# Fewer weight conversions in the first heads' turns, more in the next stage's, one normalisation on VectorE, fewer unread products

## The chip, the cores and the metric

The kernel runs on one core of a Trainium2 chip. TensorE multiplies, VectorE (DVE) and ScalarE (ACT) do element-wise work, GpSimd (POOL) does a little of it and the indirect transfers, and SyncE (SP) issues most DMA transfers. Each engine works through its own instructions in program order, and semaphores hold an instruction back until its inputs are there. The metric is the device time of one execution in microseconds (us), lower is better.

## The reference, cut to what matters

Three blocks in a row: attention with a window of 128 and four sink positions, a feed-forward block with squared relu, and a mixture of eight experts of which each token uses two.

```python
scores = scale * np.matmul(q, k.transpose(0, 1, 3, 2))      # 2 x 8 heads, 768 x 768
scores = np.where(keep, scores, -1000000000.0)              # window or sink
a = softmax(scores); x = np.matmul(a, v)                    # -> 1536 tokens x 512
h = x @ w_in; r = np.maximum(h, 0.0); g = r * r; x = g @ w_out   # 512 -> 2048 -> 512
# gate: top 2 of 8 experts per token; each expert relu(x @ w1[e]) @ w2[e]
```

The weights `w_in` and `w_out` come as float64 and are turned into float32 in the kernel by integer operations on VectorE.

## The kernel before, in words

All of attention and of the squared-relu block is in the function `fast1`. The tokens are cut into six groups of 256 (g), each with eight heads, so that there are 48 pairs of a head and a group, called heads a = 0 to 47 below. The squared-relu block of a group has eight units u of 256 hidden columns, so there are 48 of these too, n = 8g + u.

The work is laid out by hand in the order of the program. First come the **turns of the first heads**, a loop over a = 0 to 11 (lines 717 to 755). In turn a

- TensorE makes the scores of head a + 1 (line 270, tile `s`), some unread products of ones that keep it busy (line 706, their number is in W1), in every second turn the product of two earlier heads with v (`pv`, line 352, tile `o`), and the transposes of head a - 1 (lines 326 to 330, tile `pt`);
- VectorE takes masked score and maximum of head a (line 292, two instructions), in every second turn the low part of `pv`'s result (line 358), and adds and inverts the sums of head a - 1 (lines 299 and 301);
- ScalarE takes the exponentials of head a (line 295), copies the transposes of head a - 2 (line 336), multiplies head a - 1 by the inverse sums in two halves t = 0 and t = 1 (line 311; half 0 has 128 columns up to head 7, half 1 has 256, from head 8 on both have 264), and copies `pv`'s result (line 357).

H0 says by a letter for each half which engine multiplies: "a" is ScalarE, "d" is VectorE (line 313).

Then comes the **squared-relu loop** over n (line 764). In turn n TensorE makes the scores of head n + 11, in even turns `pv`, then `mm1(n + 1)` (line 425, 24 products into `h`), the transposes of head n + 10, and `mm2(n)` (line 462). In turn 5 two small transposes (line 376) and in turn 6 the sink products (line 399) stand ahead of `mm1`. `mm1(n + 1)` reads the first weights of unit n + 1 as a high part `w` and a low part `wl`:

```python
for c in range(4):
    for a, b in PASS:                  # (0, 0), (0, 1), (1, 0)
        PE.matmul(hp[:, f], w[a][:, c * 256 + f * 128:c * 256 + f * 128 + 128], x[:, b, c],
```

So the third product of each c is the one that reads `wl`. A weight tile is made in two halves; c = 0 and 1 lie in its first half, c = 2 and 3 in its second, and the ninth product of `mm1` is the first that reads the second half of `wl`.

The **conversion** of these weights fills VectorE. There are 32 halves (for each u two of `w_in` and two of `w_out`). Each takes three instructions, called steps here: line 196, line 199 and line 202. A half of `w_in` is then rounded to its high part by ScalarE (line 205) and takes one step more, the subtraction at line 180 that writes half of `wl`. That makes 14 steps a unit and 112 in all, in a fixed list; `convert(k)` issues the next k of them at the place where it stands. The step at line 202 frees the loaded half, and a load of 512 KB three halves further on is then issued on SP's queue. The low part of unit u is complete with step 14u + 10.

The tables say how many steps stand where. In turn a of the first heads C0[a] has the number ahead of the sums of head a - 1 and the number behind them (in turn 0 only the first is issued). In turns n = 0 to 7 of the squared-relu loop C1[n] has four numbers: behind the maxima, between the sum and its inverse, behind the inverse, and behind the instructions of `act(n + 1)`.

Of the kernel before, what the change touches and what calls it, by code (L numbers as in the profile page):

```python
# [34 lines left out]
def build(tc, io):  # L35
# [3 lines left out]
    with root:  # L39
# [47 lines left out]
        wk = ph1.enter_context(tc.tile_pool(name="wk", bufs=2))  # L87
        ps = psst.enter_context(tc.tile_pool(name="ps", bufs=2, space=PSUM))
        ex = fast1(tc, io, locals())
        ph1.close()  # L90
        ph2 = ExitStack()
# [9 lines left out]
def fast1(tc, io, env):  # L101
# [70 lines left out]
    def convert(count):  # L172

        for _ in range(min(count, len(todo))):
            i, c = todo.pop(0)
            name, u, hf = cvs[i]
            sl = slice(hf * 512, hf * 512 + 512)
            if c == "L":
                w = W[name, u]
                DVE.tensor_tensor(w[1][:, sl], CV.pop(i).bitcast(F32), w[0][:, sl].bitcast(F32), op=OP.subtract)  # L180
                if hf:
                    split.add((name, u))
                continue
            wd = ST[i].bitcast(I32).rearrange("p (n t) -> p n t", t=2)
            if c == "1":
                if name == "win":
                    if hf == 0:
                        W[name, u] = env["halves"]()
                    t = CV[i] = cvp.tile([128, 512], I32, name="cv", bufs=3)
                else:  # L190
                    if hf == 0:

                        RAW[name, u] = spare.tile([128, 1024], F32, name="rw0") if u == 7 else \
                            ring.tile([128, 1024], F32, name="wl")
                    t = CV[i] = RAW[name, u][:, sl].bitcast(I32)
                DVE.tensor_scalar(t, wd[:, :, 1], 0x07FFFFFF, 3, op0=OP.bitwise_and, op1=OP.logical_shift_left)
            elif c == "2":
                t = CV[i]
                DVE.scalar_tensor_tensor(t, wd[:, :, 1], -1073741824, t, op0=OP.bitwise_and, op1=OP.bitwise_or)
            else:  # L200
                t = CV[i]
                DVE.scalar_tensor_tensor(t, wd[:, :, 0], 29, t, op0=OP.logical_shift_right, op1=OP.bitwise_or)
                del ST[i]
                if name == "win":
                    ACT.copy(W[name, u][0][:, sl], t.bitcast(F32))
                elif hf:
                    made.add((name, u))
                cv_load()
# [89 lines left out]
    def norm_a(a, sm, between=0):  # L298
        DVE.tensor_scalar(sm[:, 0:2], sm[:, 0:2], 1.0e-9, None, op0=OP.add)
        convert(between)  # L300
        DVE.reciprocal(sm[:, 2:4], sm[:, 0:2])

    def norm(a, sm, how):
        g, h = divmod(a, 8)
        p = PR[a]
        for t in range(2):
            sc = sm[:, 2 + t:3 + t]
            lo, hi = span(a, t)
            pt = p[:, t, lo:hi]
            if how[t] == "a":  # L310
                ACT.activation(pt, pt, AF.Copy, scale=sc)
            else:
                (DVE if how[t] == "d" else POOL).tensor_scalar(pt, pt, sc, None, op0=OP.mult)  # L313
        if g % 3:
            if h == 0:
                PSK[g] = wk.tile([128, 2, 64], F32, name="psk", bufs=1)
            for t in range(2):
                o = 128 + 128 * t
                POOL.tensor_copy(PSK[g][:, t, h * NS:h * NS + NS], p[:, t, o:o + NS])  # L319
# [96 lines left out]
    def mm1(n):  # L416
        g, u = divmod(n, 8)
        hp = ps.tile([128, 2, 256], F32, name="h")
        assert ("win", u) in split
        x, w = XT[g], W["win", u]  # L420
        for f in range(2):
            i = 0
            for c in range(4):
                for a, b in PASS:
                    PE.matmul(hp[:, f], w[a][:, c * 256 + f * 128:c * 256 + f * 128 + 128], x[:, b, c],  # L425
                              start=i == 0, stop=i == 11)
                    i += 1
        HP[n] = hp
# [256 lines left out]

    A0 = 11
    PLAIN = tuple(range(18))
    C0 = ((1, 1),) + ((2, 1),) * 11
    H0, H1, H2 = "aa", "aa", "dd"
    C1 = ((3, 1, 4, 4),) * 8  # L690
    smv = {}
    HALF, V1 = 18, (5, 6, 7)
    W0, W1 = 20, (6, 5) + (4,) * 9

    with tc.manual_schedule():
        cvst = ExitStack()
# [20 lines left out]
        for a in range(A0 + 1):  # L717
# [15 lines left out]
            if a == 10:  # L733
                mm1(0)
            convert(C0[a][0])
            if a >= 2:
# [5 lines left out]
            if a >= 1:  # L742
                norm_a(a - 1, smv[a - 1])
                norm(a - 1, smv[a - 1], H0)
                convert(C0[a][1])
            if a in (3, 5, 7, 9):
# [17 lines left out]
        for n in range(48):  # L764
# [44 lines left out]
            if first:  # L809
                convert(C1[n][0])  # L810
            if a:
                norm_a(a, smv[a], C1[n][1] if first else 0)
            if first:
                convert(C1[n][2])
            if a:
# [28 lines left out]
            if first:  # L844
                convert(C1[n][3])
            if n + 10 < 8 * NG:
# [545 lines left out]
```

## Time and profile before

| | |
|---|---|
| time, median of 3 runs | 746.63 us (746.58 to 746.78) |
| the profiled execution | 746.56 us, of which the span of its instructions is 744.7 us |
| TensorE busy | 726.2 us (98% of the span) |
| VectorE busy | 451.4 us (61%) |
| ScalarE busy | 354.1 us (48%) |

The page cuts the span into 40 slices and gives each engine's busy share in each. TensorE is at nine tenths or more in all but the last. That row counts a product until its modelled end, so it hides short gaps; they are seen in the list of instructions in order of time. VectorE's row is at six to nine tenths in the first seven slices, which are the first heads and the first turns of the squared-relu loop, and mostly at four to six later.

### The profile page before, as it was taken

Reading aid. Unit: us, or ns where it says so; the run is one execution under the profiler, and the core shown is the slowest. Engines: PE = TensorE matmul, PEld = TensorE weight load, DVE = VectorE, ACT = ScalarE, POOL = GpSimd, SP = SyncE. Lnnn points to the kernel's source line nnn. Section 1 sums busy time; section 2 is a strip of 40 time slices with the busy share of each in tenths; the row PEclk is TensorE's granted clock in tenths of the full one; section 3 lists DMA queues with packets and bytes.
Section 4 is the critical chain, followed back from the end, with each engine's and each line's share of the span. In section 5 each row is a group of like instructions: output and inputs, shape, how many; then the busy total and the mean of one; then the engine's idle time right before and its main releaser. Section 6 shows DMA issues by size and latency. Waiting matters only on the chain. (4 is left out here: it accounts for less than half of the span.)

```text
span 744.7 us, 12224 instructions
## 1 busy us (share of the span) xinstructions
PE 726.2 (98%) x4447; PEld 631.2 (85%) x4447; DVE 451.4 (61%) x1151; ACT 354.1 (48%) x749; POOL 116.6 (16%) x274
## 2 busy tenths in 40 slices
PE   9999999999999999999999999999999999999995
PEld 4476658888988888888899978899999999999994
DVE  6878966787677758766665436444544455555411
ACT  5866566665565664554454325333443334444310
POOL 1011100012004001310212130203011110203022
PEclk9999999999999999999999999999999999999998
DMA  8757765366746324432525056636465555646133
GB/s 225 239 167 235 224 240 190 130 238 222 234 148 237 129 95 158 155 122 85 189 75 165 16 174 205 188 111 170 129 181 143 149 147 164 158 147 169 58 44 46
DMA packets 37092, 117.35 MB, mean 158 GB/s; under 512 B 5038, under 2 KB 5166, under 8 KB 36768
## 3 DMA queue, kind: packets, MB, share of 16 engines
q1 hardware_dynamic: 30800, 102.16, 42.4%
q0 software_dynamic: 5792, 13.28, 8.6%
q10 hardware_dynamic: 432, 1.05, 0.5%
q8 instruction: 37, 0.61, 0.3%
q14 instruction: 31, 0.25, 0.1%
HBM read 103.20 MB, written 24.91 MB: 172 GB/s over the span
## 5 line engine op out<-in xcount | busy, mean ns | idle before, releaser
L425 PE MATMUL h<-xt,w 128*128 128x256 f32 x768 | 143.3, 287 | 0.0
L425 PEld LDWEIGHTS h<-xt,w 128*128 128x128 f32 x768 | 119.4, 191 | 5.1 <-issue 4.2
L1077 PE MATMUL h<-xt,w 128*128 128x448 f32 (+6 forms) x448 | 120.0, 349 | 0.0
L425 PE MATMUL h<-xt,wl 128*128 128x256 f32 x384 | 108.7, 283 | 0.8 <-DVE wl L180 0.8
L470 PE MATMUL acc<-w,gt 128*128 128x512 f32 x320 | 108.3, 401 | 0.0
L1084 ACT ACTIVATE hh<-h 128x256 fp32r<-128x256 f32 (+7 forms) x60 | 29.8, 496 | 149.4 <-PE h L1077 149.4
L1085 DVE SCALAR_TENSOR_TENSOR hh<-h,hh 128x256 fp32r<-128x256 f32 (+7 forms) x60 | 33.9, 565 | 108.8 <-ACT hh L1084 107.4
L980 DVE TENSOR_TENSOR wl<-rw,w 128x1024 fp32r<-128x1024 f32 x64 | 78.4, 1225 | 32.8 <-ACT w L979 31.8
L1077 PEld LDWEIGHTS h<-xt,w 128*128 128x128 f32 x448 | 83.1, 188 | 2.2
L295 ACT ACTIVATE pr<-pr,mxall 128x264 f32<-128x264 f32 (+1 forms) x88 | 43.2, 492 | 76.9 <-DVE mxall L292 71.7
L1077 PE MATMUL h<-xt,wl 128*128 128x448 f32 (+6 forms) x224 | 78.1, 349 | 0.0
L425 PEld LDWEIGHTS h<-xt,wl 128*128 128x128 f32 x384 | 73.4, 191 | 1.0 <-DVE wl L180 1.0
L470 PEld LDWEIGHTS acc<-w,gt 128*128 128x128 f32 x320 | 59.9, 188 | 12.8 <-DVE gt L447 0.9
L979 ACT CAST w<-rw 128x1024 fp32r<-128x1024 f32 x64 | 67.1, 1048 | 4.8 <-DMA rw<-in_w 4.7
L319 POOL COPY psk<-pr 128x8 f32<-128x8 f32 x64 | 22.8, 361 | 266.3 <-DVE pr L313 138.8
L470 PE MATMUL acc<-wl,gt 128*128 128x512 f32 x160 | 62.5, 390 | 0.0
L1051 POOL DMA_INDIRECT out<-x2t,mi x15 | 22.7, 1514 | 235.6 <-DVE x2t L1129 234.4
L434 ACT ACTIVATE r<-h 128x512 f32<-128x512 f32 x48 | 28.4, 593 | 56.5 <-PE h L425 56.5
L1104 PE MATMUL acc<-hh,w 128*128 128x448 f32 (+5 forms) x192 | 54.6, 365 | 0.0
L1104 PE MATMUL s<-hh,w 128*128 128x448 f32 (+5 forms) x192 | 51.7, 350 | 0.0
L292 DVE CUSTOM_DVE_ANT_0 pr<-s,masks 128x264 f32<-128x264 f32 (+1 forms) x88 | 32.9, 408 | 24.5 <-PE s L274 18.3
L1077 PEld LDWEIGHTS h<-xt,wl 128*128 128x128 f32 x224 | 42.0, 188 | 0.8
(296 smaller groups left out, 1409.6 us busy)
## 6 DMA issues: line engine op xcount, KB each, us to landing
rw<-in_w SPq DMA_DIRECT2D x64, 512.0 KB, 3.3
qk<-in_qk SPq DMA_DIRECT2D x30, 328.0 KB, 4.8
st<-in_wout SPq DMA_DIRECT2D x16, 512.0 KB, 4.7
rw<-in_win SPq DMA_DIRECT2D x16, 512.0 KB, 4.6
rw<-in_wout SPq DMA_DIRECT2D x16, 512.0 KB, 3.9
st<-in_win SPq DMA_DIRECT2D x15, 512.0 KB, 4.7
xg<-in_xg SPq DMA_DIRECT2D x8, 924.0 KB, 6.6
xr<-xg SPq DMA_DIRECT2D x24, 231.0 KB, 4.4
```

Of the source, the lines that this page charges most:

```text
L292: DVE.tensor_tensor_reduce(pt, SB[a][t][:, lo:hi], masks[:, t if gl == 0 else 2 + t, lo:hi], scale=-0.0625 if a in PLAIN and a >= HALF els ...
L295: ACT.activation(pt, pt, AF.Exp, bias=mx, scale=-1.0, accum_out=sm[:, t:t + 1])
L319: POOL.tensor_copy(PSK[g][:, t, h * NS:h * NS + NS], p[:, t, o:o + NS])
L425: PE.matmul(hp[:, f], w[a][:, c * 256 + f * 128:c * 256 + f * 128 + 128], x[:, b, c], start=i == 0, stop=i == 11)
L434: ACT.activation(r, hp.rearrange("p a b -> p (a b)"), AF.Relu)
L470: PE.matmul(ACC[g][t], gt[:, a, f * 256 + t * 128:f * 256 + t * 128 + 128], w[b][:, f * 512:f * 512 + 512], start=u == 0 and f == 0 and i ...
L979: nc.scalar.copy(w[0], t)
L980: nc.vector.tensor_tensor(w[1], t, w[0].bitcast(F32), op=OP.subtract)
L1077: PE.matmul(hp[:, :ncol], w[a][:, o:o + 128], XT[k][b][:, c, :ncol], start=i == 0, stop=i == 11)
L1084: ACT.activation(hh[0][:, :ncol], hp[:, :ncol], AF.Relu)
L1085: DVE.scalar_tensor_tensor(hh[1][:, :ncol], hp[:, :ncol], 0.0, hh[0][:, :ncol].bitcast(F32), op0=OP.max, op1=OP.subtract)
L1104: PE.matmul(acc[:, :n], w[a][:, o + j * 128:o + j * 128 + 128], hh[b][:, :n], **st)
```

## The change

Five lines of tables in `fast1` change; no function does.

```diff
     A0 = 11
     PLAIN = tuple(range(18))
-    C0 = ((1, 1),) + ((2, 1),) * 11
-    H0, H1, H2 = "aa", "aa", "dd"
-    C1 = ((3, 1, 4, 4),) * 8
+    C0 = ((1, 1),) * 12
+    H0, H1, H2 = "da", "aa", "dd"
+    C1 = ((3, 1, 4, 5),) * 8
     smv = {}
     HALF, V1 = 18, (5, 6, 7)
-    W0, W1 = 20, (6, 5) + (4,) * 9
+    W0, W1 = 20, (6, 5, 4, 4) + (3,) * 7
```

The turns of the first heads issue 23 conversion steps in place of 34 (one in turn 0, then two in place of three in each of eleven turns). A turn of the squared-relu loop issues 13 in place of 12, so that the 112 steps end in turn 6 in both. Half 0 of heads 0 to 10 is multiplied on VectorE. From turn 4 of the first heads on three unread products stand where there were four; the last entry of W1 that is used is turn 9's, so six products go.

VectorE in turn 5 of the squared-relu loop, before. The two rows of line 180 that write `wl_968` make the low part of the unit that TensorE multiplies in this turn; line 292 is the turn's start.

```order
L180 TENSOR_TENSOR wl_968<-cv_969,w_967 128x512
L202 SCALAR_TENSOR_TENSOR cv_978<-st_934,cv_978 128x512
L196 TENSOR_SCALAR wl_1026<-st_965 128x512
L199 SCALAR_TENSOR_TENSOR wl_1026<-st_965,wl_1026 128x512
L180 TENSOR_TENSOR wl_968<-cv_978,w_967 128x512
L292 ISA pr_1042,mxall_80<-s_1038,masks_79 128x264
L292 ISA mxall_80 128x1
L292 ISA pr_1042,mxall_80<-s_1040,masks_79 128x264
L292 ISA mxall_80 128x1
L378 COPY skt_1051<-pt_1048 64x256
L202 SCALAR_TENSOR_TENSOR wl_1026<-st_965,wl_1026 128x512
```

The same place after the change; the unit's low part is now `wl_1004`.

```order
L292 ISA pr_1026,mxall_80<-s_1024,masks_79 128x264
L292 ISA mxall_80 128x1
L378 COPY skt_1035<-pt_1032 64x256
L199 SCALAR_TENSOR_TENSOR cv_1012<-st_956,cv_1012 128x512
L180 TENSOR_TENSOR wl_1004<-cv_1005,w_1003 128x512
L202 SCALAR_TENSOR_TENSOR cv_1012<-st_956,cv_1012 128x512
L299 TENSOR_SCALAR sm_1027<-sm_1027 128x2
L196 TENSOR_SCALAR wl_1044<-st_1001 128x512
L301 RECIPROCAL sm_1027<-sm_1027 128x2
L199 SCALAR_TENSOR_TENSOR wl_1044<-st_1001,wl_1044 128x512
L180 TENSOR_TENSOR wl_1004<-cv_1012,w_1003 128x512
L202 SCALAR_TENSOR_TENSOR wl_1044<-st_1001,wl_1044 128x512
```

The half that the ninth product reads stood ahead of the turn's maxima and is now its sixth step behind them.

VectorE in turn 6 before, from the maxima to the step that completes the low part (`wl_1064` before, `wl_1099` after). Line 403 adds the sink products of the same turn.

```order
L292 ISA pr_1133,mxall_80<-s_1131,masks_79 128x264
L292 ISA mxall_80 128x1
L403 TENSOR_TENSOR xraw_597<-pt_1147,xraw_597 128x512
L199 SCALAR_TENSOR_TENSOR rw0_1119<-st_1060,rw0_1119 128x512
L180 TENSOR_TENSOR wl_1064<-cv_1072,w_1063 128x512
```

VectorE at the same place after the change.

```order
L403 TENSOR_TENSOR xraw_569<-pt_1133,xraw_569 128x512
L196 TENSOR_SCALAR cv_1137<-st_1050 128x512
L199 SCALAR_TENSOR_TENSOR cv_1137<-st_1050,cv_1137 128x512
L180 TENSOR_TENSOR wl_1099<-cv_1100,w_1098 128x512
L299 TENSOR_SCALAR sm_1120<-sm_1120 128x2
L202 SCALAR_TENSOR_TENSOR cv_1137<-st_1050,cv_1137 128x512
L301 RECIPROCAL sm_1120<-sm_1120 128x2
L196 TENSOR_SCALAR rw0_1145<-st_1096 128x512
L199 SCALAR_TENSOR_TENSOR rw0_1145<-st_1096,rw0_1145 128x512
L180 TENSOR_TENSOR wl_1099<-cv_1137,w_1098 128x512
```

It was the second step of the turn and is now the seventh.

VectorE in turn 4 of the first heads before, from the maximum of head 4 to the last step of the turn.

```order
L292 ISA pr,mxall<-s,masks 128x256
L292 ISA mxall 128x1
L358 TENSOR_TENSOR xt<-o,xt 128x256
L202 SCALAR_TENSOR_TENSOR wl<-st,wl 128x512
L196 TENSOR_SCALAR wl<-st 128x512
L299 TENSOR_SCALAR sm<-sm 128x2
L301 RECIPROCAL sm<-sm 128x2
L199 SCALAR_TENSOR_TENSOR wl<-st,wl 128x512
```

VectorE in the same turn after the change.

```order
L292 ISA pr,mxall<-s,masks 128x256
L292 ISA mxall 128x1
L358 TENSOR_TENSOR xt<-o,xt 128x256
L196 TENSOR_SCALAR wl<-st 128x512
L299 TENSOR_SCALAR sm<-sm 128x2
L301 RECIPROCAL sm<-sm 128x2
L313 TENSOR_SCALAR gt<-gt,sm 128x128
L199 SCALAR_TENSOR_TENSOR wl<-st,wl 128x512
```

One step fewer stands between line 358 and the sums, and the multiplication of half 0 follows the inverse.

## Rows read from the trace of the kernel before

**Rows 1.** The page: granted TensorE clock by slice, in tenths of full speed.

```profile
PEclk9999999999999999999999999999999999999998
```

**Rows 2.** Waits of TensorE, longest total first: total us, times, longest.

```profile
PE pt L1034 <- DMA xr<-xg: 1.6, 1, 1.6
```

**Rows 3.** Instructions in order of time: start, length, what, idle before; first heads.

```profile
5.08 0.29 DVE L116 TENSOR_SCALAR r<-rel,snw 128x128 f32<-128x128 f32 x1
...
17.69 0.87 PE L352 MATMUL o<-ptt,vb 128*64 128x256 f32 x8
...
19.01 0.42 DVE L358 TENSOR_TENSOR xt<-o,xt 128x256 fp32r<-128x256 f32 x1 [0.92 <-ACT xt L357]
...
20.29 0.19 DVE L299 TENSOR_SCALAR sm<-sm 128x2 f32<-128x2 f32 x1
...
20.77 0.80 ACT L311 ACTIVATE gt<-gt,sm 128x128 f32<-128x128 f32 x2 [0.54 <-DVE sm L301]
...
21.99 0.92 PE L270 MATMUL s<-kk 64*128 64x128 f32 x4
...
22.84 1.04 PE L706 MATMUL acc<-ones 128*128 128x512 bf16 x4
...
23.81 0.87 PE L352 MATMUL o<-ptt,vb 128*64 128x256 f32 x8
...
30.46 0.87 PE L352 MATMUL o<-ptt,vb 128*64 128x256 f32 x8
...
37.06 0.87 PE L352 MATMUL o<-ptt,vb 128*64 128x256 f32 x8
```

**Rows 4.** The same view of TensorE alone, the squared-relu loop's first turns.

```profile
40.25 0.50 PE L425 MATMUL h<-xt,w 128*128 128x256 f32 x2
...
52.46 1.15 PE L270 MATMUL s<-qk 64*128 64x264 f32 x4
...
60.48 1.15 PE L270 MATMUL s<-qk 64*128 64x264 f32 x4
...
69.51 1.15 PE L270 MATMUL s<-qk 64*128 64x264 f32 x4
...
77.53 1.16 PE L270 MATMUL s<-qk 64*128 64x264 f32 x4
...
87.17 1.16 PE L270 MATMUL s<-qk 64*128 64x264 f32 x4
...
88.42 0.48 PE L425 MATMUL h<-xt,w 128*128 128x256 f32 x2
...
95.33 1.16 PE L270 MATMUL s<-qk 64*128 64x264 f32 x4
...
99.19 0.50 PE L425 MATMUL h<-xt,w 128*128 128x256 f32 x2
...
101.24 0.39 PE L425 MATMUL h<-xt,wl 128*128 128x256 f32 x1 [0.84 <-DVE wl L180]
```

**Rows 5.** The same view of VectorE, turns 3, 5 and 6 of that loop.

```profile
70.82 0.42 DVE L292 CUSTOM_DVE_ANT_0 pr<-s,masks 128x264 f32<-128x264 f32 x1
...
71.52 0.42 DVE L196 TENSOR_SCALAR cv<-st 128x512 int32<-128x512 int32 x1
...
88.03 0.43 DVE L292 CUSTOM_DVE_ANT_0 pr<-s,masks 128x264 f32<-128x264 f32 x1 [0.22 <-PE s L270]
...
89.07 0.67 DVE L202 SCALAR_TENSOR_TENSOR wl<-st,wl 128x512 int32<-128x512 int32 x1
...
99.30 0.69 DVE L403 TENSOR_TENSOR xraw<-pt,xraw 128x512 f32<-128x512 f32 x1 [1.81 <-PE pt L399]
99.90 0.68 DVE L199 SCALAR_TENSOR_TENSOR rw<-st,rw 128x512 int32<-128x512 int32 x1
100.50 0.68 DVE L180 TENSOR_TENSOR wl<-cv,w 128x512 fp32r<-128x512 f32 x1
```

**Rows 6.** Waits of VectorE in the first 110 us: total us, times, longest.

```profile
DVE cv L196 <- DMA st<-in_win: 2.9, 5, 1.1
```

## Prediction

> **What bounds the kernel now.** I read the clock row first, then the waits of TensorE, then the instructions in order of time in the two stages that the tables touch. TensorE runs at its upper level, 2.4 GHz, from end to end by the page [rows 1], and its longest wait behind the start is 1.6 us [rows 2]. From the squared-relu loop on its products stand back to back, so whatever shifts TensorE there shifts the end by as much. Two stretches decide what the change is worth.
>
> In the first heads TensorE is not the bound. A loop runs over two turns and three engines: `pv` at 17.69, its copy on ScalarE, the low part on VectorE at 19.01, two conversion steps, the sums at 20.29, the two multiplications on ScalarE at 20.77, the transposes, the scores at 21.99, four unread products at 22.84, and the next `pv` at 23.81 [rows 3]. That is one loop of 6.12 us; the next two take 6.65 and 6.60 (to 30.46 and 37.06). `mm1(0)` starts at 40.25 [rows 4].
>
> In the squared-relu loop TensorE is the bound, and VectorE keeps just behind it. Turns 1 to 5 start with the scores at 52.46, 60.48, 69.51, 77.53, 87.17 and end with turn 6's at 95.33, so they take 8.02, 9.03, 8.02, 9.64 and 8.16 us [rows 4]. VectorE's part of a turn cannot start ahead of the scores: its maximum waits for them and begins 0.86 us behind their start (87.17 to 88.03, with TensorE named as the releaser [rows 4, 5]). All conversion steps that stand behind the maximum in the program begin later than that. One wait shows what this can cost: in turn 6 the ninth product of `mm1(7)` stood idle for 0.84 us for line 180 on VectorE [rows 4], which ran from 100.50 to 101.18 as the turn's second step behind line 403 [rows 5].
>
> **The change part by part: the first heads.** On the loop above one step of about 0.60 us goes (between line 358 and the sums stand 1.28 us before: 0.34 for line 358 itself and two steps). The two multiplications on ScalarE took 0.80 us together [rows 3]; half 0 now runs on VectorE beside half 1 on ScalarE, which takes some 0.40 off. The trace has no multiplication by a column on VectorE here; the nearest rows are line 116, 0.29 us for 128x128 with a column as its operand [rows 3], and line 196, 0.42 us for 512 columns [rows 5]. I take 0.29 for 128 columns and 0.33 for 264; it is hidden beside half 1. One unread product goes: four of them hold the place from 22.84 to 23.81 [rows 3], so about 0.21 us. The sum is 1.2 us a loop if nothing else comes in its way, 3.6 us for three loops.
>
> Something does come. VectorE has in two turns four maxima (2 x 0.70 [rows 5]), line 358 (0.34), twice the sums and the inverse (0.3 each with their latency), twice the new multiplication (0.25), and four steps (some 2.1 us), 4.9 to 5.2 us together; TensorE has some 5.0. A loop can therefore hardly fall under 5.1 us. Following the three engines in order through the three loops with these lengths I get 5.2, 5.4 and 5.8 us in place of 6.1, 6.65 and 6.6: **2.8 us earlier** at `mm1(0)`. As bounds I keep 2.0 (VectorE's longer chain adds a latency in each turn) and 3.6 (the full sum).
>
> On the unread products: the row shows a granted clock of nine tenths or more in each of the first slices [rows 1], with four of these products in each turn. The Trainium skill (page "TensorE: Matmul & The Clock Gate", section "The HAM clock gate (the "warmup" mystery)") says that the throttled clock is the default and that activity releases it. By that rule taking six products out could cost more than their time; by the row it gives 0.21 us each. I go by the row, since the other products of these turns stay and move closer together.
>
> **The squared-relu turns.** Eleven steps fewer are done when turn 0 begins (23 in place of 34), and one more a turn makes it up only by turn 6. The half that `mm1(n + 1)`'s ninth product reads is complete with step 14(n + 1) + 10. Before turn n, 34 + 12n steps were issued before the change, 23 + 13n after. So this half was step 2n - 10 of turn n, which is in an earlier turn up to n = 5 and the second one in turn 6; it becomes step **n + 1 of turn n** in every turn. It stands behind the maximum, hence behind the scores of the same turn, and TensorE comes to the ninth product about 1.1 us after the first one of `mm1` (in turn 6, first at 99.19; the wait begins at 101.24 - 0.84 = 100.40 [rows 4]). With the maxima over at 0.86 + 0.70 = 1.56 us from the turn's start, step lengths of 0.42 (line 196) and 0.60 (the others: 99.30, 99.90 and 100.50 are 0.60 apart [rows 5]), 0.68 for the last, and 0.1 each for the sum and its inverse, the half is there at
>
> - turn 1: 1.56 + 0.60 + 0.68 = 2.8 us; turn 2: 1.56 + 0.42 + 0.60 + 0.68 = 3.3;
> - turn 3: 1.56 + 0.60 + 0.42 + 0.60 + 0.1 + 0.68 = 4.0; turn 4: 1.56 + 2 x 0.60 + 0.42 + 0.60 + 0.2 + 0.68 = 4.7;
> - turn 5: the maxima and line 378 end at 88.03 to 89.07 = 1.04 behind the maximum's start [rows 5], so 0.86 + 1.04 + 3 x 0.60 + 0.42 + 0.60 + 0.2 + 0.68 = 5.6.
>
> From the ninth product to the next turn's scores TensorE needs 95.33 - 88.42 - 1.1 = 5.8 us [rows 4]. The new turns are thus 8.6, 9.1, 9.8, 10.5 and 11.4 us against 8.02, 9.03, 8.02, 9.64 and 8.16: **6.5 us more**. In turn 6 line 403 waits for the sink products, as before, and began 99.30 - 95.33 = 3.97 us into the turn [rows 4, 5]; some 0.7 of that was a late copy for `pv`, which a longer turn 5 covers, so 3.3. Then 0.60 for line 403, two steps of 0.42, four of 0.60, 0.2 and 0.68 make 8.0 us against 5.85 (101.18 - 95.33): **2.2 us more**, or 2.9 if the copy is late again. Together 8.7; 8.3 if the sums and inverses cost nothing beside the steps, 9.4 with the late copy.
>
> VectorE has 13 steps, the maxima and the sums in a turn, some 8.3 us, and starts 0.86 into it; the first two turns, 8.6 and 9.1, are shorter than the 9.2 that this makes, so it is up to half a microsecond late there, and more where a step waits for its load. Five such waits make 2.9 us, the longest 1.1 [rows 6]. Eleven steps later means three or four loads of 512 KB that move out of the first heads into these turns, on the same SP queue, ahead of some loads of q and k whose buffers are free by then. I add 1.1 us for this, with 0 and 2 as ends. ScalarE gets the roundings of line 205 later in a turn, ahead of the copy of the transposes; the next reader is `pv` a turn later, and the longer turns cover it. The last three steps now end about a microsecond ahead of `mm2(7)`, which reads them; no cost, unless loads are later than I think.
>
> **Sum.** The profiled execution took 746.56 us, 0.07 under the median of 746.63. -2.8 + 8.7 + 1.1 = +7.0 us, so **753.6 us** on the median. The bounds of the terms give +4.7 (-3.6 + 8.3) to +9.4 (-2.0 + 9.4 + 2.0), or 751.3 to 756.0. Behind turn 6 I find nothing that takes a delay back: there the steps are over, and TensorE runs on.
>
> **Rivals.**
> *The low part is there in time.* If VectorE were so early that step n + 1 ended before the ninth product, only the gain would be left, and turn 6's 0.84 us would go too: 746.6 - 2.8 - 0.84 = 743.0 us, faster. It decides at 2.2 us from the scores in odd turns (1.08 for the scores and 1.1 to the ninth product) and some 3.2 in even ones. For it speaks that TensorE shows no such wait in turns 1 to 5 today; against it that none of these steps stood behind the maximum there, and that five or six steps cannot run in under 0.7 us.
> *The gain and the stalls cancel.* If turns 1 to 4 cost nothing, because VectorE passes the short steps faster, turns 5 and 6 alone cost 3.2 + 2.2 against the gain of 2.8 to 3.6 and 1.3 us of late copies in turns 4 and 6 that vanish: 746.6 to 747.5 us, no change.
> *The clock falls in the new waits.* In turns 5 and 6 TensorE would stand twice for some 2 us in 5, longer than any wait before (1.6 us at the upper level [rows 1, 2]). At 1.2 GHz the 5.8 us behind the ninth product would double; half of that in two turns is 5.8 us: 759 us. That page's rule, that activity releases the clock and idleness withdraws it, speaks for it; the trace shows no fall.
>
> **How the numbers follow.** I give the forecast 0.70 (751 to 757), a lesser loss between 748.2 and 751 another 0.06, the clock's fall 0.10 (756.5 to 763), the cancelling 0.07 and the early low part 0.07. A range from 751.0 to 757.5 holds the first and some of the third, about eight in ten. What a measurement of this kernel can tell from no change is about 0.2%, 1.5 us. The chances are 0.08 faster (0.07 and a sliver of the cancelling), 0.06 the same, and 0.86 slower.
>
> **What would show it.** In the profile of the changed kernel: `mm1(0)` starts near 37.5 us; TensorE waits for line 180 in each of turns 1 to 6, least in turn 2, and 3 us or more in turns 5 and 6, where the third product waits too, some 11 us in all; the scores of turns 1 to 6 are at about 49.7, 58.4, 67.5, 77.5, 88.2 and 99.8; VectorE's line 292 keeps beginning 0.86 us behind the scores. It is wrong if these waits are short or absent, if `mm1(0)` starts before 36.5 or after 38.5, or if the granted clock drops under nine tenths in the slices around 95 to 110 us.

## The result and the profile after the change

| | before | after |
|---|---|---|
| time, median (lowest to highest) | 746.70 us (746.58 to 748.25) | 758.99 us (757.50 to 759.64) |
| profiled execution, its span | 746.56 us, 744.7 us | 758.89 us, 757.1 us |
| ratio after to before | | 1.0148, interval 1.0130 to 1.0166 |

The change makes the kernel slower by 1.5%, some 12.3 us. The direction was forecast. The size was not: 753.6 us was predicted, in a range of 751.0 to 757.5. The time lies where the prediction put its rival of the falling clock, 759 us, to which it gave a tenth. The sign of being wrong that the prediction named for it, a granted clock under nine tenths around 95 to 110 us, came true.

The page's row of the granted TensorE clock, after the change, answers to [rows 1]:

```profile
PEclk9999988999999999999999999999999999999998
```

Before, every slice but the last stood at nine tenths or more. Now the sixth and the seventh, which are 95 to 133 us, stand at eight. A fall that lasts a few microseconds, as the one in turn 3 below, can be too short to show in a slice of 19 us. The waits of TensorE after the change, longest total first (total us, times, longest), answer to [rows 2]:

```profile
PE h L425 <- DVE wl L180: 6.1, 7, 2.0
PE h L425 <- ACT w L205: 2.5, 4, 0.9
PE o L352 <- ACT ptt L336: 1.2, 2, 1.0
...
PE pt L1034 <- DMA xr<-xg: 0.5, 1, 0.5
```

The first two rows are the stalls in `mm1`, 8.6 us in place of one of 0.84 [rows 4], where the prediction had some 11; in the third `pv` waits for its transposes. The last is the wait that was the longest before, 1.6 us [rows 2].

Three places tell the rest. **The first heads** gained what was forecast. TensorE in order of time after the change (start, length, what), against [rows 3] and [rows 4]:

```profile
17.48 0.87 PE L352 MATMUL o<-ptt,vb 128*64 128x256 f32 x8
22.75 0.87 PE L352 MATMUL o<-ptt,vb 128*64 128x256 f32 x8
28.14 0.87 PE L352 MATMUL o<-ptt,vb 128*64 128x256 f32 x8
33.93 0.87 PE L352 MATMUL o<-ptt,vb 128*64 128x256 f32 x8
37.10 0.50 PE L425 MATMUL h<-xt,w 128*128 128x256 f32 x2
```

From `pv` to `pv` the loops now take 5.27, 5.39 and 5.79 us, and `mm1(0)` starts at 37.10 in place of 40.25, 3.15 us earlier. Some 0.2 us of that were there at the first scores already (7.52 in place of 7.72), ahead of anything that the change touches; in the runs below these scores start anywhere from 6.8 to 8.4 us.

**The squared-relu turns** lose it five times over. The scores after the change, in the same view, where the last row is the first work behind turn 6 that has a form of its own (line 274):

```profile
49.29 1.15 PE L270 MATMUL s<-qk 64*128 64x264 f32 x4
58.19 1.15 PE L270 MATMUL s<-qk 64*128 64x264 f32 x4
68.90 1.15 PE L270 MATMUL s<-qk 64*128 64x264 f32 x4
80.46 1.15 PE L270 MATMUL s<-qk 64*128 64x264 f32 x4
91.07 1.15 PE L270 MATMUL s<-qk 64*128 64x264 f32 x4
104.16 1.15 PE L270 MATMUL s<-qk 64*128 64x264 f32 x4
124.93 1.05 PE L274 MATMUL s<-kk,qs 128*128 128x264 f32 x4
```

The same work before the change:

```profile
111.41 1.05 PE L274 MATMUL s<-kk,qs 128*128 128x264 f32 x4
```

| turn | 1 | 2 | 3 | 4 | 5 | 6 (to line 274) | sum |
|---|---|---|---|---|---|---|---|
| before, us [rows 4] | 8.02 | 9.03 | 8.02 | 9.64 | 8.16 | 16.08 | 58.95 |
| forecast, without loads | 8.6 | 9.1 | 9.8 | 10.5 | 11.4 | 18.3 | 67.7 |
| after | 8.90 | 10.71 | 11.56 | 10.61 | 13.09 | 20.77 | 75.64 |

These turns take 16.7 us more. With the 3.15 us of the first heads that leaves 13.5, and 1.1 us come back at line 1034, whose wait was for a transfer: 12.4 us, the difference of the two spans. Turns 1 and 4 came out as forecast; turns 2, 3, 5 and 6 did not.

**Turn 5** shows why. VectorE there, after the change (start, length, what, idle time before), against [rows 5]:

```profile
91.92 0.43 DVE L292 CUSTOM_DVE_ANT_0 pr<-s,masks 128x264 f32<-128x264 f32 x1 [1.56 <-PE s L270]
...
93.57 0.68 DVE L180 TENSOR_TENSOR wl<-cv,w 128x512 fp32r<-128x512 f32 x1
...
95.90 0.68 DVE L180 TENSOR_TENSOR wl<-cv,w 128x512 fp32r<-128x512 f32 x1
```

The maximum begins 0.85 us behind the scores, and the second half of the low part, the last row, is there at 96.58, 5.5 us behind them; 5.6 was forecast. VectorE had even stood idle for 1.56 us ahead of the maximum. It is late by the place of its steps, not by their number: the order experiment below shows it. TensorE in the same turn:

```profile
91.07 1.15 PE L270 MATMUL s<-qk 64*128 64x264 f32 x4
...
94.30 0.39 PE L425 MATMUL h<-xt,wl 128*128 128x256 f32 x1 [1.50 <-DVE wl L180]
...
95.55 0.50 PE L425 MATMUL h<-xt,w 128*128 128x256 f32 x2 [0.51 <-ACT w L205]
96.64 0.39 PE L425 MATMUL h<-xt,wl 128*128 128x256 f32 x1 [0.58 <-DVE wl L180]
96.86 0.40 PE L425 MATMUL h<-xt,w 128*128 128x256 f32 x2
...
97.72 0.63 PE L425 MATMUL h<-xt,w 128*128 128x256 f32 x2
...
98.36 0.63 PE L425 MATMUL h<-xt,w 128*128 128x256 f32 x2
```

The three waits are the forecast ones, on the third, seventh and ninth product. Behind them something new appears. A pair of products on `w` takes 0.63 us where it took 0.40, and three products take 0.64 (97.72 to 98.36). From the last wait, 96.64, to the next scores at 104.16 it is 7.52 us; the forecast had 5.8, from before. The granted clock says what it is. Stretches after the change (from:to and length in us; busy time of PE, PE's weight loads, DVE, ACT and POOL; granted clock as a share of full speed; DMA share; GB/s):

```profile
70.00:73.00 3.00, 1.51 (x10) 1.10 (x9) 2.97 (x11) 1.62 (x5) 0.00 (x0) 1.00 0.75 238
73.00:77.00 4.00, 4.00 (x21) 4.00 (x22) 3.86 (x7) 1.54 (x4) 0.93 (x2) 0.57 0.73 219
...
86.00:88.00 2.00, 2.00 (x17) 1.76 (x16) 1.92 (x4) 0.67 (x2) 0.03 (x1) 1.00 0.61 197
...
95.00:97.00 2.00, 0.91 (x6) 0.66 (x6) 2.00 (x5) 1.35 (x3) 1.00 (x2) 1.00 0.50 147
97.00:101.00 4.00, 4.00 (x21) 3.83 (x20) 3.62 (x7) 1.09 (x2) 0.24 (x1) 0.57 0.72 226
...
112.00:118.00 6.00, 5.76 (x23) 5.25 (x24) 1.78 (x4) 2.57 (x6) 0.83 (x2) 0.51 0.59 214
```

In three stretches, each right behind the waits of turns 3, 5 and 6, the clock is at or near its lower level, 1.2 GHz, while TensorE is busy all or nearly all of the time. The ninth products of turns 3, 4 and 6, each behind the last wait of its turn:

```profile
72.94 0.39 PE L425 MATMUL h<-xt,wl 128*128 128x256 f32 x1 [0.54 <-DVE wl L180]
...
85.09 0.39 PE L425 MATMUL h<-xt,wl 128*128 128x256 f32 x1 [0.57 <-DVE wl L180]
...
112.24 0.58 PE L425 MATMUL h<-xt,wl 128*128 128x256 f32 x1 [0.28 <-DVE wl L180]
```

From there to the next mark it took 7.52 us in turn 3 (72.94 to 80.46) and 7.52 in turn 5. In turn 4, where the ninth product waits as well but the granted clock stays at 1.00, it took 5.98 (85.09 to 91.07). In turn 6 it took 12.69 us (112.24 to 124.93), against 10.17 before (101.24 [rows 4] to 111.41). That is 1.5 + 1.5 + 2.5, some **5.6 us** of clock.

### The profile page after: what moved, and what is told of

It is laid out like the page before. It is cut to its first block, busy times and chain, and to the rows that moved or that the text cites. A ratio compares the mean times of both kernels' runs of the same rounds, so it can differ in the third digit from the quotient of the medians.

```text
span 757.1 us, 12212 instructions
## 1 busy us (share of the span) xinstructions
PE 732.2 (97%) x4441; PEld 636.5 (84%) x4441; DVE 454.9 (60%) x1162; ACT 351.6 (46%) x738; POOL 116.6 (15%) x274
## 3 DMA queue, kind: packets, MB, share of 16 engines
q10 hardware_dynamic: 432, 1.05, 0.5%
## 5 line engine op out<-in xcount | busy, mean ns | idle before, releaser
L425 PE MATMUL h<-xt,w 128*128 128x256 f32 x768 | 147.7, 292 | 2.5 <-ACT w L205 2.5
L425 PEld LDWEIGHTS h<-xt,w 128*128 128x128 f32 x768 | 122.3, 196 | 8.4 <-issue 3.9
L425 PE MATMUL h<-xt,wl 128*128 128x256 f32 x384 | 111.3, 290 | 6.1 <-DVE wl L180 6.1
L1077 PEld LDWEIGHTS h<-xt,w 128*128 128x128 f32 x448 | 83.1, 188 | 2.2
L425 PEld LDWEIGHTS h<-xt,wl 128*128 128x128 f32 x384 | 75.2, 196 | 7.6 <-DVE wl L180 7.6
L1077 PEld LDWEIGHTS h<-xt,wl 128*128 128x128 f32 x224 | 42.0, 188 | 0.8
```

What stands on the lines that cost most here:

```text
L1077: PE.matmul(hp[:, :ncol], w[a][:, o:o + 128], XT[k][b][:, c, :ncol], start=i == 0, stop=i == 11)
```

## The experiments

The theory to be tried: the line 180 that `mm1` reads now stands behind the turn's maximum, TensorE waits for it, and the waits take the clock down. Its rivals are these. The clock falls because unread products are gone. VectorE has too much to do in these turns, wherever the steps stand. The slow products behind the waits are something other than a result of the waits. For the first heads it is open which of the three edits brings the gain. All experiments start from the changed kernel. The times of before with which they are compared are those of the same chip.

**The steps alone.** The multiplication and the unread products are as before; only C0 and C1 are changed.

```diff
-    H0, H1, H2 = "da", "aa", "dd"
+    H0, H1, H2 = "aa", "aa", "dd"
-    W0, W1 = 20, (6, 5, 4, 4) + (3,) * 7
+    W0, W1 = 20, (6, 5) + (4,) * 9
```

> C0 and C1 of the change alone; H0 and W1 stay as before (both halves on ScalarE, four unread products a turn). If the waits come from where line 180 stands behind the maxima, they are all here again: TensorE waits for line 180 and line 205 in turns 1 and 3 to 6 for some 8.5 us, the granted clock drops in turns 3, 5 and 6, and only the gain of the first heads is smaller (some 1.8 us in place of 3.1): about 760 us. If the six unread products that are left out make the clock fall, it stays up here: about 754.5 us.

Measured: 762.96 us (759.72 to 763.13), ratio 1.0188 (1.0150 to 1.0225), with a span of 761.2 us. The clock row of its page:

```profile
PEclk9999988999999999999999999999999999999998
```

The waits of TensorE (total us, times, longest):

```profile
PE h L425 <- DVE wl L180: 6.3, 7, 2.0
PE h L425 <- ACT w L205: 2.5, 4, 0.9
PE pt L1034 <- DMA xr<-xg: 2.3, 1, 2.3
```

The waits of `mm1` and the two lower slices are those of the change, with all unread products in place. So the fall doesn't come from their removal: that rival is out. The three loops of the first heads took 17.28 us (17.77 to 35.05) against 19.37 before and 16.45 after the change, so the steps bring 2.1 of the 2.9 us. Three of its four runs are some 4 us slower than the whole change, the fourth by 0.7. Of the 4.1 us between the spans 0.8 are these loops and 1.8 the longer wait at line 1034, behind which the clock fell once more, to 0.50 and then 0.67 (the same view as above, the granted clock ahead of the last two numbers; its first stretch):

```profile
453.00:455.00 2.00, 2.00 (x6) 1.57 (x5) 1.15 (x2) 0.48 (x1) 0.00 (x0) 0.50 0.00 0
```

**The multiplication as before, the rest changed.**

```diff
-    H0, H1, H2 = "da", "aa", "dd"
+    H0, H1, H2 = "aa", "aa", "dd"
```

> The change with both halves on ScalarE again (H0 alone undone). From the scores of head 2 to those of head 11 the change takes 24.86 us, the kernel before 27.80, C0 and C1 alone 25.71. If the six products are worth 0.21 us each on the path, and the multiplication on VectorE little, this is about 25.1; if the multiplication is what brings the rest, it is near 25.7. Waits and clock in the squared-relu turns as in the change: 759 to 760 us.

Measured once: 761.66 us, span 759.9. From the scores of head 2 to those of head 11 it took 25.06 us, as in the first case. The loops took 16.63 us (17.24 to 33.87), so the multiplication on VectorE is worth 0.2 us and the six unread products the other 0.6 or so of the 0.8 above. The waits in the squared-relu loop came back (6.6 us for line 180). In turn 3 the two waits were 0.94 and 1.36 us and the turn took 13.58 us in place of 11.56: the price of such a turn is not a fixed one.

**The steps of the first heads as before.** Thirteen steps a turn stay in the squared-relu loop.

```diff
-    C0 = ((1, 1),) * 12
+    C0 = ((1, 1),) + ((2, 1),) * 11
```

> The change with C0 as before (three steps a turn of the first heads); 13 steps a turn, half 0 on VectorE and three unread products stay. If the place of line 180 is the cause, it now stands in an earlier turn everywhere, TensorE waits for it nowhere, the clock stays up, and the two other edits show their gain of the first heads (about 0.6 us a loop, 1.8 us) and the 0.84 us of turn 6: about 744 us. If thirteen steps a turn are too many for VectorE, waits for line 180 and for the copy of the transposes remain: over 746.7 us.

Measured: 747.62 us (746.78 to 749.34), ratio 1.0004 (0.9990 to 1.0017), no change. No wait for line 180 is left, so these waits come from the eleven missing steps. But the gain that was expected did not come. The loops took 18.98 us (18.41 to 37.39) against 19.37: without fewer steps the other two edits bring little. And turn 2 took 13.16 us, 4.1 more than before, for a wait of another kind. The wait on TensorE (start, length, what, idle before), and two rows of ScalarE that explain it:

```profile
64.44 1.83 PE L352 MATMUL o<-ptt,vb 128*64 128x256 f32 x10 [1.93 <-ACT ptt L336]
```

```profile
63.29 0.62 ACT L205 CAST w<-cv 128x512 fp32r<-128x512 f32 x1 [2.64 <-DVE cv L202]
63.81 0.58 ACT L336 COPY ptt<-pt 128x512 f32<-128x512 f32 x1
```

The stretch behind it, with the granted clock ahead of the last two numbers:

```profile
64.00:68.00 4.00, 3.56 (x18) 3.05 (x19) 3.62 (x12) 3.34 (x9) 0.00 (x0) 0.58 0.72 231
```

`pv` waits for the copy of the transposes (line 336). That copy stands on ScalarE behind the rounding of line 205, which had waited for 2.64 us for the twelfth step of turn 1 on VectorE. That is the order in which the program issues them: the last steps of a turn, `convert(C1[n][3])`, ahead of the copy. After the change the same pair cost turn 2 a wait of 1.02 us; the prediction had seen the roundings move ahead of the copy and given them no cost. A single wait of 1.93 us took the clock down too.

**TensorE kept busy in the waits.** Unread products of ones are put ahead of the products that wait, with their results in columns of the PSUM tile that the sum under way doesn't use; the table says how many stand ahead of which product i of unit n.

```diff
+    FILL = {(2, 0, 8): 5, (4, 0, 6): 8, (4, 0, 8): 4, (5, 0, 6): 4, (5, 0, 8): 4,
+            (6, 0, 2): 13, (6, 0, 6): 4, (6, 0, 8): 4, (7, 0, 2): 17, (7, 0, 6): 4, (7, 0, 8): 3}
...
+                    for _ in range(FILL.get((n, f, i), 0)):
+                        PE.matmul(hp[:, 1], env["ones"], env["ones"][:, None, :].to_broadcast([128, 2, 128]),
+                                  start=True, stop=True, skip_group_check=True)
```

> The change, with unread products of ones put into the waits of mm1 (5 in turn 1, 12 in turn 3, 8 in turn 4, 21 in turn 5, 24 in turn 6; each about 0.11 us, a little less than the wait in all). The waits stay, but TensorE works through them. If the fall of the granted clock is a part of the loss by itself, it does not fall, and the slow stretches behind the waits (about 1.6 us in turn 3, 1.7 in turn 5, 2.5 in turn 6) come back: about 753 us, which is the loss that I had forecast. If the clock costs nothing, 759 us.

Measured: 754.28 us (752.27 to 754.56), ratio 1.0073 (1.0043 to 1.0102). The clock row is back at nine tenths in every slice but the last, and turn 5 took 11.54 us in place of 13.09. Here each of these products starts a sum of its own in the same bank, by which the hidden values of these units come out different; the next kernel lets them add to what stands there.

```diff
-                                  start=True, stop=True, skip_group_check=True)
+                                  start=False, stop=True, skip_group_check=True)
```

> The change with the same numbers of unread products in the waits of mm1 as in the run before, now added onto columns that the second half's first product overwrites. If the granted clock's fall is a loss of its own, the waits stay as long, the clock stays at its upper level in every slice, and the loss against the kernel before is some 6 to 7 us in place of 12: the turns 3, 5 and 6 get back 1.6, 1.7 and 2.5 us. If the clock had cost nothing, the loss stays at 12 us.

Measured: 753.43 us (752.47 to 754.35), ratio 1.0063 (1.0039 to 1.0087), span 750.7. The first products of turn 5 in order of time (lines stand five further down here; 428 is the filling):

```profile
90.56 1.59 PE L428 MATMUL h<-ones 128*128 128x256 bf16 x13
92.22 0.38 PE L430 MATMUL h<-xt,wl 128*128 128x256 f32 x1
...
94.56 0.39 PE L430 MATMUL h<-xt,wl 128*128 128x256 f32 x1
94.78 0.40 PE L430 MATMUL h<-xt,w 128*128 128x256 f32 x2
```

A stretch of the same kernel (the granted clock is the number ahead of the last two):

```profile
90.00:100.00 10.00, 9.74 (x59) 6.87 (x59) 8.55 (x20) 5.08 (x12) 1.24 (x2) 1.00 0.57 193
```

TensorE comes to its ninth product 5.57 us behind the scores (88.99 to 94.56), exactly as after the change (91.07 to 96.64): the useful work waits as long as it did. But the clock stays up, the pair behind it takes 0.40 us, and the turn is over 11.55 us behind its start. The six turns took 8.88, 10.04, 10.85, 10.63, 11.55 and 18.25 us, 70.2 together against 75.6. So the clock is a result of the waits, and it is worth 5.4 us by these turns (5.6 by the rows above; by the ratios, less exactly, 0.85% or 6.3 us). Turns 5 and 6 gave back 1.5 and 2.5, as by the rows. Turn 3 gave back only 0.7, since its ninth product came 0.8 us later behind the scores than after the change (4.87 against 4.04), and turn 2 was 0.7 shorter. What is left, 0.63% or some 4.7 us, is the waiting itself less the gain.

**The order of the halves.** The last two experiments leave the number of steps a turn and put the steps that are due first in front. The first weights of unit u + 1 are converted ahead of the second weights of unit u (line numbers are one higher).

```diff
-    cvs = [(n, u, hf) for u in range(8) for n in ("win", "wout") for hf in range(2)]
+    seq = [("win", 0)] + [x for u in range(7) for x in (("win", u + 1), ("wout", u))] + [("wout", 7)]
+    cvs = [(n, u, hf) for n, u in seq for hf in range(2)]
```

> The change, with the list of halves in another order: the first weights of unit u + 1 ahead of the second weights of unit u, so that line 180 comes seven steps earlier; as many steps, in the same places. If the place of line 180 is the cause, its waits are gone in turns 1 to 6 and the clock stays up, and the gain of the first heads (3.1 us) and of turn 6 (0.84 us) is left: 742.7 us, up to 744.5 if VectorE with its 13 steps makes other readers late. If the cause is the number of steps or of loads in these turns, the time stays near 757 to 759 us.

Measured: 744.68 us (743.01 to 747.18), ratio 0.9959 (0.9943 to 0.9976). All steps of the change stay where they are, thirteen a turn, and only what they work on is another. Of the waits for line 180 (here 181) one of 0.23 us is left, and the clock row is at nine tenths in every slice but the last. So VectorE did not have too much to do, and the place of the low part decides. What waits now is `pv`, and in turn 5 the small transposes, for the copy of the transposes (2.3 us in four waits), the cause seen in turn 2 above. The next kernel issues that copy earlier, by one line that moves:

```diff
+            if n + 10 < 8 * NG:
+                trans_b(n + 10)
             if first:
                 convert(C1[n][3])
-            if n + 10 < 8 * NG:
-                trans_b(n + 10)
```

> The order of halves with the first weights of unit u + 1 ahead, and the copy of the transposes (line 336) issued ahead of the last five steps of a turn, so that on ScalarE it no longer stands behind a rounding that waits for VectorE's last steps. If the waits of pv come from that place, TensorE's waits for line 336 in turns 1 to 7 (1.1 us in turns 4 and 5 of the run with this order alone) are gone and the time is about 1 us under that run's, some 4 us under the kernel before. If they come from late loads alone, they stay and the time is the same as that run's.

Measured: 743.88 us (743.25 to 744.25), ratio 0.9936 (0.9915 to 0.9957). It is faster than the kernel before by 0.6% and than the changed one by 2%. VectorE in its turn 5:

```profile
84.51 0.68 DVE L181 TENSOR_TENSOR wl<-cv,w 128x512 fp32r<-128x512 f32 x1
...
86.77 0.69 DVE L181 TENSOR_TENSOR wl<-cv,w 128x512 fp32r<-128x512 f32 x1
87.38 0.43 DVE L293 CUSTOM_DVE_ANT_0 pr<-s,masks 128x264 f32<-128x264 f32 x1
```

TensorE in the same turn:

```profile
83.77 1.15 PE L271 MATMUL s<-qk 64*128 64x264 f32 x4
85.93 0.38 PE L377 MATMUL pt<-ident,psk 128*64 128x128 f32 x2 [1.00 <-ACT ptt L337]
...
87.52 0.39 PE L426 MATMUL h<-xt,wl 128*128 128x256 f32 x1 [0.26 <-DVE wl L181]
```

Both halves of the low part now stand ahead of the maximum (line 293), and the ninth product loses 0.26 us in place of 2.6 in three waits. The waits for the copy were expected to go, and they did not: 1.8 us in three of them are left. Turn 4's went (0.52 us with the order alone); turn 5's became 1.00 in place of 0.60, and turn 6's 0.65 in place of 1.05. There the copy no longer stands behind the last rounding, but ScalarE still comes to it late, since a rounding ahead of it had waited 2.64 and 3.81 us for VectorE. So the line that moves is worth less than expected, and 743.88 against 744.68 us is not clear of the noise. With the order of the halves the fewer steps of the first heads keep their worth.

**Four steps more in the first heads.** Between the two schedules: the last four turns of the first heads keep three steps.

```diff
-    C0 = ((1, 1),) * 12
+    C0 = ((1, 1),) * 8 + ((2, 1),) * 4
```

> The change with four more steps in the first heads (two ahead of the sums in turns 8 to 11), so that the low part is complete with step n - 3 of turn n in place of n + 1. By the place of line 180 TensorE then waits for it in turn 5 only (0.9 us) and in turn 6 about as long as before the change; some 1 us of the gain of the first heads goes: about 745.5 us, and 747.5 if pv waits a microsecond or two for its copy as with the old C0. If the number of steps in a turn is what counts, it is the same as in the change and the time stays over 755 us.

Measured: 749.66 us (748.73 to 757.44), ratio 1.0033 (1.0006 to 1.0061). The waits for line 180 fell from seven with 6.1 us to two with 2.2, in turns 5 and 6, as the place of the steps has it. But the time did not fall below that of before. In turn 5 two waits of 0.9 us, for the copy of line 336 and for line 180, again took the clock down (0.72 in the stretch behind them, from 92 to 96 us), and the wait at line 1034 grew to 2.4 us. I had counted neither. Fewer such waits cost less, but the gain is not had back step by step.

## Why the prediction was right and wrong

**The first heads: right.** Loops of 5.2, 5.4 and 5.8 us were forecast, 5.27, 5.39 and 5.79 measured; 2.8 us were forecast for `mm1(0)`, 3.15 came, of which the loops are 2.9. Following the three engines in order gave this; the plain sum of what the edits take off, 3.6, would have been too much. The two prices that no row of before showed were near: the multiplication on VectorE takes 0.29 us for 128 columns, as assumed, and 0.36 for 264 (0.33 was assumed). On the unread products the row was right: the clock in the first 40 us stayed at 1.00 without six of them. What the prediction weighed by the Trainium skill (page "TensorE: Matmul & The Clock Gate", section "The HAM clock gate (the "warmup" mystery)"), that the clock could fall there for want of activity, did not show.

**The place of the low part: right.** It is complete 2.9, 4.0, 4.6, 5.5 and 8.0 us behind the scores in turns 1, 3, 4, 5 and 6, and 2.8, 4.0, 4.7, 5.6 and 8.0 were forecast. In turn 2 it came at 4.5 in place of 3.3, but TensorE was later still there. The rival in which it is there in time is out. The order experiment gives what that rival stood for, by another way: its 743.0 us were the price of the gain without the waits, and 744.68 and 743.88 are close to it.

**Turn 2 and the loads: a small miss.** Turn 2 took 10.71 us where its sum had 9.1. Around its start VectorE waited 0.76 and 0.48 us for loads, and `pv` 1.02 us for the copy of line 336 behind ScalarE's rounding. The prediction named that order and gave it no cost, since "the longer turns cover it"; turn 1 was not long enough. The 1.1 us that it allowed for loads were too little: with the clock kept up, turns 2 and 3 are together 2.0 us over their sums, which is the upper end of that term.

**The clock: the step that failed.** The sum took the 5.8 us behind the ninth product as they were before the change, at the upper level, in all turns. They were 7.5 us in turns 3 and 5, and turn 6 lost 2.5. The prediction had the mechanism as a rival, with a place (turns 5 and 6) and a price, 5.8 us; the price measured is 5.4 to 5.6. That the two agree is in part luck: the rival had 2.9 us in each of two turns, and the runs show 1.5 in turn 3, 1.5 in turn 5 and 2.5 in turn 6. What was wrong is its chance, and a sum that put it at nothing. It was held at one tenth since "the trace shows no fall": one wait of 1.6 us at the upper level [rows 2]. That row is a lone wait, and it was compared with each new wait by itself. But the prediction's own working had TensorE stand twice for some 2 us in 5, with only a few products between. No row of before showed such a stretch, so the rows spoke neither way. The term should have had both ends, 0 and 5.8 us, in the sum's bounds, and the range would have reached 759 at least.

**Behind turn 6: a miss that helped.** "I find nothing that takes a delay back" was wrong. The products of line 1034 waited 1.6 us for a transfer [rows 2] and only 0.5 after the change; 1.1 us of the delay went there. This was luck: the wait does not follow how late a kernel comes, as it was 2.3 us with the steps alone, 2.4 with four steps more and 0.6 in the fastest kernel, and the runs don't show why.

Together: 753.6 forecast, 0.35 less for the first heads, 1.1 less at line 1034, and 6.9 more in the turns (16.7 in place of 9.8, of which 5.4 to 5.6 are the clock's) make 759.0, the measured 758.99.

**A sum that does not come out.** The rival in which gain and stalls cancel was put at 746.6 to 747.5 us. Its own terms, 3.2 + 2.2 less 2.8 to 3.6 and less 1.3, make 747.1 to 747.9, and the late copy of turn 6 is in two of them. The forecast does not rest on it.

## What to carry to other kernels

A step on an in-order engine is due at its reader's time, and what counts is what stands ahead of it in the program. What moved steps cost is not their length but how far behind such a point they fall, here the maximum that waits for the scores of the same turn. Before any step is moved, list for each the product that reads it first; here another order of the same steps, two lines of the program, kept the gain without the stalls. And where a sum finds several waits close together on TensorE, the clock behind them belongs in the forecast itself: here it cost some 5.5 us beside waits of 8.6.

## What the runs showed of the hardware

The granted clock fell behind stretches of waits that were short one by one. Behind 0.95 and 0.54 us in turn 3, and behind 1.50, 0.51 and 0.58 us in turn 5, it was at 0.57 over the next 4 us, though TensorE was busy all that time. With 0.49 and 0.57 us in turn 4 it stayed at 1.00, and the lone wait of 1.02 us in turn 2 did nothing. Alone, a wait of 1.93 us (turn 2, with the old steps in the first heads) and one of 2.27 us (line 1034, the steps alone) took it down, and one of 2.44 us at the same line, with four steps more, did not:

```profile
438.00:440.00 2.00, 0.00 (x0) 0.00 (x0) 0.00 (x0) 0.00 (x0) 0.00 (x0) 1.00 0.75 233
440.00:442.00 2.00, 1.66 (x11) 1.38 (x12) 0.47 (x1) 0.93 (x2) 0.63 (x5) 1.00 0.10 37
442.00:444.00 2.00, 2.00 (x11) 1.62 (x10) 1.11 (x3) 0.24 (x1) 0.00 (x0) 1.00 0.00 0
```

So the length of a wait alone doesn't decide, and these runs don't settle what does. Unread products in the waits kept the clock up each time. The Trainium skill (page "TensorE: Matmul & The Clock Gate", section "A second HAM failure mode: psum-queue depth-cycling") tells of a kernel in which many short idles between groups of products make the clock go up and down; turns 3 and 5 here agree with it.

The unread products that began a sum of their own in other columns of the same PSUM bank changed the sum that was under way in it (the output of that kernel is off by a relative 0.41), and those that added did not. The Trainium skill (page "PSUM — Partial Sum Buffer", section "The four PSUM rules") says that the first product of a sum clears the marks of the whole bank, by which a sum under way in it starts afresh; the two filling experiments agree.
